# Transposes in 64 x 64 tiles and a static task graph in a talking-heads attention and feed-forward kernel

## The chip, the cores and the metric

The kernel runs on one core of a Trainium2 chip. The metric is device time in microseconds (us) of one execution, the lower the better; of several runs the median counts. TensorE is called PE in the profile (its weight loads PEld), VectorE DVE, ScalarE ACT, GpSimd POOL, SyncE SP.

## What is computed

Attention with "talking heads" (heads are mixed before and after the softmax), then a feed-forward layer with a squared ReLU:

```
q, k, v: (8, 12, 448, 64)    w_pre, w_post: (12, 12)    w_in: (768, 2048)    w_out: (2048, 768)
scores = q @ k^T / sqrt(64)                         # per batch and head
scores = einsum('bhij,hg->bgij', scores, w_pre)     # pre-mix over heads
attn   = softmax(scores, axis=-1)
attn   = einsum('bhij,hg->bgij', attn, w_post)      # post-mix over heads
x      = (attn @ v) as (8*448, 768)                 # tokens by heads*64
out    = relu(x @ w_in)**2 @ w_out                  # (3584, 768), float32
```

## The kernel before

**Stages of one batch.** POOL's queue issues the loads of q, k and v from HBM; they are cast to bf16 on the way. A token is number 4p + r: partition p of 112, place r of 4, so one source row of a head is 4 x 64 floats, 1024 bytes. TensorE transposes q and k (L635) with the identity as the moving operand: a task per pair of heads, 16 transposes of 112 x 64, the two heads of a pair on the two column halves of the array. The result is evicted to qkt, 64 features x 448 tokens, two heads on top of each other. QK (L768) gives scores of 12 chunks of 10 queries at a time, evicted to stage; a pair of heads is two matmuls of 448 columns, on the two row halves of the array. A move on SP's queue (L821, "rel", dring<-stage) rearranges each chunk of 10 queries x 12 heads into 120 partitions, in a ring of 12 slots. The pre-mix (L861) multiplies two chunks by a block matrix wk1 in four 64 x 64 tiles. ACT takes the exponential with the row sum (L884), DVE the reciprocal (L897), POOL folds it into the post weights wk2s (L905). The post-mix (L951) has the exponentials as stationary operand, 112 keys and 16 columns of padding at a time, and so gives the mixed attention with keys on partitions (a2t, evicted by L369 and L370). AV (L1023) sums over the four places r of the keys, 112 partitions each. Feed-forward: L1088 (F1) with ReLU at L1121 or L1122 and the square at L1131 (POOL or DVE), then L1180 (F2), eviction to osb, output by POOL's queue (L1245).

The first 100 queries of batch 0 take another way ("direct", L714): DVE and POOL scale the transposed q by w_pre (L686), and one matmul sums over heads; no move is needed.

**Tilings of the array.** QK, post-mix, F1 and F2 use two row halves ("row"), the pre-mix four quadrants ("quad"), transposes and AV two column halves ("cols"), direct and warm-up matmuls the full array ("full").

**What sets the order.** A planner in the kernel's own Python (class _Plan) runs while the program is built. TensorE's order is the string ORDER, written out by hand: each digit takes the next unit of one of ten streams (0 transposes, 1 QK, 2 pre-mix, 3 post-mix, 4 AV, 5 direct, 6 and 7 F1, 8 and 9 F2). The other engines take the ready task that can start first, with priorities; evictions go to ACT or DVE, whichever would end first by the planner's costs, squares to DVE or POOL. What comes out is a fixed order for each engine, with semaphores between them. PSUM has 8 banks that the planner hands out, oldest free first. Tasks appear in Python as the plan proceeds: a unit's "needs" and "go" create its followers, and the loads of batch 2 and later are released by a count of chunks (paced, GAP = 3). Transfers are reckoned with one time for loads and one for moves, and a fixed time that a move takes from running loads (STEAL). In the first 60 us warm-up matmuls (L598) are put where the planner sees a gap of TensorE, sized by that gap.

An F1 unit is half of a phase (6 matmuls), an F2 unit a quarter (8 matmuls); two phases make a group that holds two banks.

On POOL's queue at the start, the first four loads have a lower priority number than the identity (init2, L384), the other four a higher one; h0 is 0, 4, 8 or 10:

```
t_init2 = add("init2", POOL, fn_init2, [t_init], {POOL: (310.0, 400.0)}, -1e7 + 6)
-1e7 + h0 if b == 0 else b * 1000.0 - 1700.0 + h0
```

Of the kernel before, what the change touches and what calls it, by code (L numbers as in the profile page):

```python
# [6 lines left out]
AF = mybir.ActivationFunctionType  # L7
ALU = mybir.AluOpType
# [10 lines left out]
MODE_SWITCH = 108  # L19
ACT_BIAS = 14.5  # L20
STEAL = 560.0
INF = float("inf")
MERGE = False
ORDER = (
    "011051051501555115555555555551155551155551323332323233112111123323234322666767377667766662"
    "266766377662372777737733021112201121313313114181667666676627777776636666226687727738377277"
    "381281818118822188328338328388231991191192293991932242206163666361266616366362267667373777"
    "377220277117777177383383811411811866226688226686636633266661761716717277117777332777722779"
    "393329391191291912193820208322838338318318128224119122919339239121911913933230224333662206"
    "116616116626612263663636362277217737711177337173712277722778338224118118382218883932291919"  # L30
    "139139119329323818338222840081183181816362266662236663612266366363622771177173713171777222"
    "777737337382240028338318138118181228881238183181183282228993919339224339229199191391391192"
    "299392266326623636361316661161661622006316773227777331777171173771722277842833883118811822"
    "881832283893388138824229939222991939366116616362226677377636116166613636171711732777228737"
    "833772277421818118338118228838222883883228893391193911932299192239933919222941911933961163"
    "366226677166237716622667713771636226167373773722737738181838324228888338382228899822898398"
    "399339936677646777667676677676667686776867676777868777676777888667667766877667766999889889"
    "999999989999888"
# [12 lines left out]
class _Task:  # L51
# [3 lines left out]
                 "done", "bias", "sync")  # L55

    def __init__(self, name, engine, fn, deps, after, cost, prio, sem, seminc, mode, dma):
# [18 lines left out]
        self.done = False  # L76
        self.bias = 0.0
        self.succs = []
        self.avail = 0.0


class _Unit:

    __slots__ = ("mode", "go", "needs", "nbanks")

    def __init__(self, go, needs, nbanks=0, mode=None):
        self.mode = mode
        self.go = go
        self.needs = needs
        self.nbanks = nbanks  # L90


class _Plan:


    def __init__(self, nbanks):
        self.tasks = []
        self.ready = []
        self.free = {PE: 0.0, ACT: 1300.0, DVE: 400.0, POOL: 1400.0, SP: 800.0}
        self.per_engine = {e: [] for e in ENGINE_NAMES}  # L100
        self.committed = []
        self.streams = []
        self.mode = None
        self.load_free = 0.0
        self.move_free = 0.0
        self.loads = []
        self.bank_users = {i: [] for i in range(nbanks)}
        self.bank_age = {i: i for i in range(nbanks)}
        self.taken = set()
        self.age = nbanks  # L110
        self.keep_warm = lambda gap: None

    def add(self, name, engine, fn, deps=(), cost=None, prio=0.0, sem=None, seminc=0,
            mode=None, after=(), dma=None):
        t = _Task(name, engine, fn, deps, after, cost, prio, sem, seminc, mode, dma)
        t.order = len(self.tasks)
        self.tasks.append(t)
        t.nwait = 0
        for d in t.deps + t.after:
            if d.done:  # L120
                t.avail = max(t.avail, d.end + SEM_LAT if d in t.deps else 0.0)
            else:
                t.nwait += 1
                d.succs.append(t)
        if engine == PE:
            assert t.nwait == 0
            start = max(self.free[PE], t.avail)
            if t.mode != self.mode:
                start += MODE_SWITCH
                self.mode = t.mode  # L130
            self._commit(t, PE, start)
        elif t.nwait == 0:
            self.ready.append(t)
        return t

    def _commit(self, t, e, start):
# [4 lines left out]
        if t.dma:  # L141
            kind, service, piece = t.dma
            if kind == "load":
                self.load_free = max(self.load_free, start + 1200.0) + service
                t.end = max(start + held, self.load_free) + 1600.0
                self.loads.append(t)
            else:
                at = start + 900.0
                behind = self.load_free - at
                if behind > 0:  # L150
                    at += min(behind, 2000.0)
                    service += min(behind, 12.0 * max(
                        [45.0] + [x.dma[2] for x in self.loads if x.end > at]))
                    self.load_free += STEAL
                    self.loads = [x for x in self.loads if x.end > max(at, self.move_free)]
                    for x in self.loads:
                        x.end += STEAL
                self.move_free = max(self.move_free, at) + service
                t.end = self.move_free + 2200.0
        t.done = True  # L160
        self.per_engine[e].append(t)
        self.committed.append(t)
        for s in t.succs:
            s.nwait -= 1
            if t in s.deps:
                s.avail = max(s.avail, t.end + SEM_LAT)
            if s.nwait == 0:
                self.ready.append(s)

# [3 lines left out]
    def find(self, n, now):  # L173
        best = sorted((max(self.bank_time(i), now), self.bank_age[i], i)
                      for i in self.bank_users if i not in self.taken)
        if len(best) < n:
            return INF, ()
        return best[n - 1][0], [x[2] for x in best[:n]]

    def take(self, n):  # L180
        _, got = self.find(n, self.free[PE])
        self.taken.update(got)
        return got, [t for i in got for t in self.bank_users[i]]

    def give(self, banks, users):
        for i in banks:
            self.taken.discard(i)
            self.bank_users[i] = list(users)
            self.age += 1
            self.bank_age[i] = self.age  # L190

    def next_unit(self, order, at):
        if at >= len(order):
            return None
        s = self.streams[int(order[at])]
        u = s[0]
        needs = u.needs()
        if needs is None:
            return None
        now = self.free[PE]  # L200
        est = max([now] + [t.end + SEM_LAT if t.done else INF for t in needs if t is not None])
        if u.nbanks:
            est = max(est, self.find(u.nbanks, now)[0])
        if u.mode != self.mode:
            est = max(est, now + MODE_SWITCH)
        return (est, u, s) if est < INF else None

    def run(self, order=""):
        at = 0
        while True:  # L210
# [10 lines left out]
            f = self.next_unit(order, at)  # L221
            if f is not None and (best is None or f[0] <= best[0]):
# [1151 lines left out]
```

## Time and profile before

| | us |
|---|---|
| median of 3 runs | 564.76 (559.62 to 566.79) |
| the profiled execution's own time | 557.64 |
| its span, first to last instruction | 555.9 |
| PE busy | 523.0 |
| ACT busy | 428.7 |
| DVE busy | 380.2 |
| POOL busy (its DMA issues counted) | 249.0 |
| mean granted TensorE clock | 0.983 |

Busy times are unions of instructions, and the ends of matmuls are modelled, so start-to-start distances in the timeline say more about what a matmul costs than its own duration. In a line of a group, the name is line, engine, operation and "out<-in"; "idle before" is the engine's idle time in front of the group's instructions and what ended it. Digits of the clock row are tenths of full speed in 40 equal slices.

### The profile page before, as it was taken

To read this page: it belongs to the slowest core of one execution; us is meant where nothing else is said; L and a number is where in the kernel's file an instruction comes from. 1 tells how busy PE (TensorE), PEld (TensorE's weight loads), DVE (VectorE), ACT (ScalarE), POOL (GpSimd) and SP (SyncE) were. 2 spreads that over 40 slices of the span, in tenths; PEclk is the share of its full clock that TensorE was granted. 3 is DMA by queue.
4 is the path that set the end of the run, shared out by engine and by line. 5 is a ranking of instruction groups with operands and counts; after the bars stand their busy time and mean duration, and the time that the engine had idled before them with its cause. 6 is when DMAs were issued, how large, how long until landed. Compare 5 with 4: busy or idle time off the path is not lost.

```text
span 555.9 us, 22831 instructions
## 1 busy us (share of the span) xinstructions
PE 523.0 (94%) x9479; PEld 328.3 (59%) x9479; DVE 380.2 (68%) x872; ACT 428.7 (77%) x1212; POOL 249.0 (45%) x441
## 2 busy tenths in 40 slices
PE   7979999999599999999999989999999999999994
PEld 3436675687376564566557555566446554558872
DVE  5776866777297878876888757965597757834430
ACT  2877977998499989897888969888888987884220
POOL 7973546355383447622763534324432326522001
PEclk8989999999899999999999989999999999999998
DMA  8999999953976899746896897435834558342013
GB/s 106 173 228 229 162 166 176 215 124 49 173 161 139 163 161 169 148 97 125 147 186 117 145 186 162 87 58 125 168 56 89 133 122 157 63 99 59 3 31 86
DMA packets 95878, 72.85 MB, mean 131 GB/s; under 512 B 6192, under 2 KB 93440, under 8 KB 95776
## 3 DMA queue, kind: packets, MB, share of 16 engines
q0 software_dynamic: 49504, 33.43, 38.8%
q1 hardware_dynamic: 46128, 37.85, 29.9%
q8 instruction: 77, 1.26, 0.9%
q14 instruction: 25, 0.20, 0.1%
q10 hardware_dynamic: 144, 0.10, 0.1%
HBM read 45.70 MB, written 11.01 MB: 102 GB/s over the span
## 4 chain that ended last, share of the span: by engine, by line
PE 78%; DMA 9%; ACT 5%; DVE 3%; SPq 2%; issue 1%; POOL 0%; POOLq 0%; ACTq 0%
PE ps L1180 25%; PE ps L1088 23%; DMA dring<-stage 8%; PE ps L861 7%; PE ps L1023 7%; PE ps L951 6%; PE ps L768 5%; PE ps L635 3%; ACT pring L884 3%; SPq L821 2%; ACT stage L369 2%; DMA kraw<-in_k_dram 1%; DVE a2t L370 1%; DVE h1t L1122 1%; DVE h2t L1131 1%
## 5 line engine op out<-in xcount | busy, mean ns | idle before, releaser
L884 ACT ACTIVATE pring<-ps 128x448 bf16<-128x448 f32 x360 | 191.8, 553 | 22.3 <-PE ps L861 19.4
L1088 PE MATMUL ps<-xt,w_in_sb 64*128 64x448 bf16 (+2 forms) x2112 | 171.8, 299 | 1.9 <-PE ps L861 0.7
L1180 PE MATMUL ps<-w_out_sb,h2t 64*128 64x384 bf16 x1792 | 172.5, 324 | 0.0
L905 POOL TENSOR_TENSOR wk2s<-wk2b,rinv 128x120 bf16<-128x120 bf16 (+1 forms) x179 | 69.9, 392 | 159.6 <-DVE rinv L897 159.0
L370 DVE CAST a2t<-ps 112x480 bf16<-112x480 f32 (+1 forms) x196 | 120.7, 638 | 20.4 <-PE ps L951 19.1
L370 DVE CAST stage<-ps 120x448 bf16<-120x448 f32 (+2 forms) x186 | 108.7, 614 | 26.8 <-PE ps L768 20.3
L1088 PEld LDWEIGHTS ps<-xt,w_in_sb 64*128 64x128 bf16 x2112 | 95.2, 94 | 48.1 <-PE ps L861 5.3
L369 ACT ACTIVATE stage<-ps 120x448 bf16<-120x448 f32 (+3 forms) x186 | 94.5, 553 | 26.9 <-PE ps L768 21.7
L1180 PEld LDWEIGHTS ps<-w_out_sb,h2t 64*128 64x128 bf16 x1792 | 81.2, 94 | 54.5 <-issue 7.7
L369 ACT ACTIVATE a2t<-ps 112x480 bf16<-112x480 f32 (+1 forms) x172 | 93.8, 576 | 12.2 <-PE ps L951 10.6
L1131 POOL TENSOR_TENSOR h2t<-h1t 128x448 bf16<-128x448 bf16 (+2 forms) x101 | 75.7, 759 | 52.1 <-ACT h1t L1121 34.6
L884 ACT ACTIVATION_READ_ACCUMULATOR pring<-ps 128x1 f32 x360 | 78.3, 218 | 0.0
L951 PEld LDWEIGHTS ps<-wk2s,pring 60*128 60x128 bf16 x2880 | 59.8, 94 | 26.2 <-issue 2.6
L861 PE MATMUL ps<-dring,wk 64*64 64x448 bf16 (+1 forms) x700 | 58.0, 368 | 15.8 <-DMA dring<-stage 10.6
L1122 DVE TENSOR_SCALAR h1t<-ps 128x448 bf16<-128x448 f32 (+2 forms) x103 | 49.4, 496 | 29.7 <-PE ps L1088 28.7
L951 PE MATMUL ps<-wk2s,pring 60*128 60x60 bf16 x2880 | 66.8, 188 | 2.5 <-POOL wk2s L905 0.8
L1245 POOL DMA_DIRECT2D out_dram<-osb x54 | 33.7, 629 | 75.5 <-DVE osb L370 44.1
L768 PE MATMUL ps<-qkt 64*128 64x448 bf16 (+2 forms) x372 | 60.5, 356 | 2.2 <-DVE qkt L370 0.9
L897 DVE RECIPROCAL rinv<-rowsum 128x2 f32<-128x2 f32 (+1 forms) x184 | 29.0, 158 | 41.1 <-ACT pring L884 40.5
L1121 ACT ACTIVATE h1t<-ps 128x448 bf16<-128x448 f32 (+2 forms) x73 | 31.5, 441 | 26.1 <-PE ps L1088 25.8
L861 PEld LDWEIGHTS ps<-dring,wk 64*64 64x64 bf16 (+1 forms) x700 | 17.2, 104 | 46.6 <-issue 17.3
L1023 PE MATMUL ps<-a2t,vraw 112*64 112x220 bf16 (+1 forms) x768 | 41.5, 266 | 0.0
(50 smaller groups left out, 361.6 us busy)
## 6 DMA issues: line engine op xcount, KB each, us to landing
dring<-stage SPq DMA_DIRECT2D x342, 105.0 KB
vraw<-in_v_dram POOLq DMA_DIRECT2D x24, 224.0 KB, 6.6
qraw<-in_q_dram POOLq DMA_DIRECT2D x23, 224.0 KB, 6.8
kraw<-in_k_dram POOLq DMA_DIRECT2D x23, 224.0 KB, 8.1
w_in_sb<-in_moe_w_in_dram POOLq DMA_DIRECT2D x8, 384.0 KB, 15.0
w_out_sb<-in_moe_w_out_dram POOLq DMA_DIRECT2D x12, 256.0 KB, 37.7
out_dram<-osb POOLq DMA_DIRECT2D x8, 336.0 KB, 4.1
out_dram<-osb POOLq DMA_DIRECT2D x8, 288.0 KB, 4.2
```

Source lines behind the costliest of these rows:

```text
L369: return eng.activation(o, i_, AF.Copy)
L370: return eng.tensor_copy(o, i_)
L768: r_ = eng.matmul(ps[0:m, banks[par], 0:S], qkt[r0:r0 + 64, pb, p, 0, i0:i0 + m], qkt[r0:r0 + 64, pb, p, 1, :], start=True, stop=True,)
L861: r_ = eng.matmul(ps[64 * y:64 * y + 64, banks[x], 0:S], wk1[64 * x:64 * x + 64 - R0 * x, :], dring[64 * x:64 * x + 64 - R0 * x, (g0 + y) ...
L884: return eng.activation(pring[:, pr, 0:S], ps[:, bank, 0:S], AF.Exp, accum_out=rowsum[:, pr, :])
L905: return eng.tensor_tensor(wk2s[:, p0:p0 + n, :], i0.to_broadcast([128, n, PR]), rinv[:, p0:p0 + n, :].to_broadcast([128, n, PR]), ALU.mult)
L951: r_ = eng.matmul(pout(banks[x], jb, y, n), pring[64 * x:64 * x + PR, pr + y, jb * JB:jb * JB + 128], wk2s[64 * x:64 * x + PR, pr + y, :], ...
L1023: r_ = eng.matmul(ps[kk * 64:kk * 64 + 64, bank, x * n:(x + 1) * n], vraw[:, h, r, :], a2t[half][:, r, h, a0:a0 + n], start=(r == 0), stop ...
L1088: r_ = eng.matmul(ps[:, banks[x], 0:n], w_in_sb[64 * y:64 * y + 64, ft, t * 128:(t + 1) * 128], xt[64 * y:64 * y + 64, ft, c0:c1], start=( ...
L1122: return eng.tensor_scalar(h1t[:, s, 0:n], ps[:, bank, 0:n], 0.0, None, op0=ALU.max)
L1131: return eng.tensor_tensor(h2t[:, t16, o0:o0 + n], h1t[:, s, 0:n], h1t[:, s, 0:n], ALU.mult)
L1180: r_ = eng.matmul(ps[:, banks[hh], 0:FH], h2t[64 * y:64 * y + 64, t16, col:col + 128], w_out_sb[64 * y:64 * y + 64, t16, hh * FH:(hh + 1) ...
```

## The change

*Layout.* A token is number 7p + t: partition p of 64, place t of 7. The loads of q and k put heads 0 to 5 on partitions 0 to 63 and heads 6 to 11 on 64 to 127, two heads a load, with source rows of 7 x 64 floats (1792 bytes); v has places 0 to 3 on the lower and 4 to 6 on the upper partitions. In the program that is built, 144 loads of q, k and v are issued where there were 74. A transpose task holds four heads: 56 transposes of 64 x 64, in waves of four quadrants, so its tiling is "quad". The transposed keys are put in the order of POS, so that the post-mix can take 128 keys (two places t) as one stationary operand without padding; AV sums over 128 partitions, and one of the eight half-blocks of v is zero. QK always takes 128 queries. The output goes out in two pieces of 64 tokens for each tile.

*Planner.* All tasks are created before planning, banks belong to a group; the costs of TensorE's units are new constants; transfers are planned as two queues that share the DMA engines in proportion to their packets; a task's instructions are counted in blocks of 256, and a block that would be needed less than 4.0 us after the one before makes the task longer in the plan. The order of loads of later batches is set by "after" (planned after a given pre-mix), which sets an order and no semaphore.

*Units and order.* An F1 unit is a whole phase (12 matmuls), an F2 unit half a phase (16); ORDER is a new string. The matmuls of all kinds but the transposes (768 to 1344) and warm-up (27 to 40) keep their numbers. In the built programs, 49 of the full-width squares on POOL become 33 and 31 on DVE become 47. On POOL the identity comes behind all twelve loads of batch 0, whose numbers are -1e7 + 0, 2 and 4.

The diff's core:

```diff
-MODE_SWITCH = 108
+MODE_SWITCH = 106.0
-STEAL = 560.0
+BLOCK = 256
+FETCH = 4000.0
+DMA_START = {"move": 1420.0, "load": 1350.0}
+DMA_END = {"move": 1850.0, "load": 1700.0}
 ORDER = (
...
+    def fetch_wait(self, t, start):
+        before = self.instrs // BLOCK
+        after = (self.instrs + t.instrs) // BLOCK
+        if after == before:
+            return 0.0, None
+        part = (after * BLOCK - self.instrs) / t.instrs
+        at = start + part * t.cost[PE][0]
+        return max(0.0, self.fetched - at), at
...
-    RJ = 4
-    JB = S // RJ
+    PJ = 64
+    NT = S // PJ
+    NS = 4
+    POS = (1, 3, 5, 0, 2, 4, 6)
...
+    QUADS = ((0, 0), (1, 1), (0, 1), (1, 0))
...
-        qraw = sb("qraw", [JB, H, RJ, D], DT.bfloat16)
+        qraw = sb("qraw", [128, H // 2, NT, D], DT.bfloat16)
...
+        def load_qk(b, a, x, u, deps, after, prio):
+            raw, src = ((qraw, q), (kraw, k))[x]
+
+            def fn(eng, en):
+                i_ = bass.AP(src.tensor, (b * H + u * NP + 2 * a) * S * D,
+                             [[NT * D, PJ], [S * D, 2], [1, NT * D]])
+                eng.dma_start(raw[64 * u:64 * u + 64, 2 * a:2 * a + 2, :, :], i_).then_inc(
+                    sem_qk[a].handle, 16)
+
+            return plan.add("ldqk%d_%d_%d_%d" % (b, a, x, u), POOL, fn, deps,
+                            {POOL: (725.0, 0.0)}, prio, sem_qk[a], 16, after=after,
+                            dma=("load", 710.0, 88.0))
...
-                        for i, src in enumerate((qraw, kraw)):
-                            for r in range(RJ):
-                                for kk in range(2):
-                                    r_ = eng.transpose(
-                                        ps_bf[kk * 64:kk * 64 + 64, bank,
-                                              i * S + r * JB:i * S + (r + 1) * JB],
-                                        src[:, 2 * p + kk, r, :],
-                                        ident[0:JB, 0:JB],
-                                    )
...
-                               c_mm(2 * RJ, JB, 10.0), 0, "cols")
+                    for i, src in enumerate((qraw, kraw)):
+                        for t in range(NT):
+                            o = i * S + (POS[t] if i else t) * PJ
+                            for u, c in QUADS:
+                                r_ = eng.transpose(
+                                    ps_bf[64 * c:64 * c + 64, g.banks[u], o:o + PJ],
+                                    src[64 * u:64 * u + 64, 2 * a + c, t, :],
+                                    ident[64 * u:64 * u + 64, 64 * u:64 * u + 64],
+                                )
...
+                t_tr = unit(s_T, "tr%d_%d" % (b, a), fn_tr, qk_tasks[(b, a)] + [t_init2],
+                            14 * 32.0 + 36.0, "quad", g, 8 * NT)
...
-                         {SP: (815.0, 0.0)}, g * 1.0, sem_dsl[slot], 16, dma=("move", 620.0, 0.0))
+                         {SP: (815.0, 0.0)}, g * 1.0, sem_dsl[slot], 16, dma=("move", 470.0, 54.0))
...
+                    for s in range(NS):
+                        j0 = (2 * s + 1) * PJ % (NT * PJ)
+                        o0 = (y * NS + s) * PR
...
+                                pring[64 * x:64 * x + PR, pr + y, j0:j0 + 2 * PJ],
```

## The prediction

> **What bounds the kernel now.** I read the page first, then the waits of TensorE, then single instructions in the timeline, then stretches of the start. The page's busy shares, its clock row and one DMA queue (packets, MB, share of the engines):
>
> ```profile
> PE 523.0 (94%) x9479; PEld 328.3 (59%) x9479; DVE 380.2 (68%) x872; ACT 428.7 (77%) x1212; POOL 249.0 (45%) x441
> PEclk8989999999899999999999989999999999999998
> q8 instruction: 77, 1.26, 0.9%
> ```
>
> TensorE is the bound in nearly every slice; ACT and VectorE have a quarter to a third of their time free. So the end moves by what TensorE no longer does, plus what it no longer waits for. Its waits, longest in total first (us in total, times, longest):
>
> ```profile
> PE ps L861 <- DMA dring<-stage: 10.6, 5, 5.8
> PE ps L861 <- ACT pring L884: 2.9, 3, 1.1
> PE ps L635 <- DMA kraw<-in_k_dram: 1.9, 1, 1.9
> PE ps L951 <- POOL wk2s L905: 0.8, 2, 0.4
> ```
>
> Half of the roughly 22 us of idle is five waits of the pre-mix for the on-chip move (dring<-stage). They cost twice: after the longest the granted clock is halved. Two stretches (us, busy by engine, then PEclk):
>
> ```profile
> 142.00:149.00 7.00, 1.26 (x16) 0.49 (x13) 1.20 (x6) 2.19 (x8) 2.42 (x5) 0.96 1.10 173
> 149.00:152.00 3.00, 2.98 (x28) 1.73 (x30) 0.00 (x0) 1.16 (x4) 0.00 (x0) 0.53 0.79 179
> ```
>
> The same halving stands at 36 to 39 us (0.50) and 322.4 to 326 (0.53), each behind such a wait: about 1.4, 1.5 and 1.7 us lost, 4.6 us together. Waits on the move with their cold clock are thus 15.2 us.
>
> What a unit of work costs on TensorE, from its timeline (start, us, then the group):
>
> ```profile
> 172.17 0.39 PE L951 MATMUL ps<-wk2s,pring 60*128 60x60 bf16 x16
> 172.41 0.82 PE L1180 MATMUL ps<-w_out_sb,h2t 64*128 64x384 bf16 x8
> 173.16 0.38 PE L861 MATMUL ps<-dring,wk 64*64 64x448 bf16 x4
> 173.47 0.39 PE L635 MATMUL ps<-ident,qraw 112*64 112x112 bf16 x8
> 173.69 0.36 PE L635 MATMUL ps<-ident,kraw 112*64 112x112 bf16 x8
> 173.89 0.36 PE L635 MATMUL ps<-ident,qraw 112*64 112x112 bf16 x8
> ...
> 176.39 0.82 PE L1180 MATMUL ps<-w_out_sb,h2t 64*128 64x384 bf16 x8
> 177.05 0.39 PE L951 MATMUL ps<-wk2s,pring 60*128 60x60 bf16 x16
> 177.37 0.57 PE L861 MATMUL ps<-dring,wk 64*64 64x448 bf16 x8
> 177.87 0.82 PE L1180 MATMUL ps<-w_out_sb,h2t 64*128 64x384 bf16 x8
> ```
>
> Read from start to start. Eight transposes (four pairs) take 0.20 us, 0.049 a pair. An output unit of eight followed by its own kind of tiling takes 0.66 (176.39 to 177.05), but 0.75 in front of the pre-mix (172.41 to 173.16): a change of the array's tiling costs 0.09. Two pre-mixes take 0.50, less 0.09 that is 0.205 each, for 448 columns that four tiles stream at once. A post-mix of 16 takes 0.24 where no tiling changes, 8 pairs of 0.030.
>
> **Transposes.** Before: 768, 384 pairs at 0.049, 18.9 us, all on TensorE's path. After: 1344 in 336 waves of four. No row has a 64-column wave. Streaming 64 columns at the pair's rate (112 columns in 0.049 less 0.0025) is 0.027, so 0.029 is the low end: 9.8 us. The high end is two tiles at a time, like the post-mix's pairs of 60 columns, 0.060 a wave: 20.2 us. The new planner holds 14 x 32 + 36 ns for a task, 0.0346 a wave. Its other constants agree with the rows above (205 ns a pre-mix, 28 ns a post pair, 164 ns an output pair where the rows have 165), and the pre-mix shows four tiles at once; so I take 24 x 0.484 = 11.6 us: minus 7.3 (minus 9.1 to plus 1.3).
>
> [...]
>
> **Changes of tiling.** Counted in the orders of the two built programs, without the full-array ones: 243 before, 192 after, since transposes now share the pre-mix's tiling and units are longer. 51 x 0.09 = minus 4.6. Full-array changes go from 26 to 45 and idle-filling warm matmuls from 27 to 40, all in the first 60 us, where they stand in front of waits: 0 to 13 x 0.19 (a 448-column matmul, as a QK pair takes) + 19 x 0.09 = 4.2 if the waits aren't there; I take 1.0.
>
> **The start.** The identity is made on POOL, in its queue behind the first four loads; in the new order it stands behind all twelve. Now:
>
> ```profile
> 1.37 0.84 POOL L513 DMA_DIRECT2D qraw<-in_q_dram  x1 [0.86 <-POOLq L1359]
> 4.38 0.34 POOL L384 TENSOR_SCALAR_AFFINE_SELECT ident<-ident 128x128 bf16<-128x128 bf16 x1
> 5.33 0.66 POOL L513 DMA_DIRECT2D kraw<-in_k_dram  x1
> 8.15 0.39 PE L635 MATMUL ps<-ident,qraw 112*64 112x112 bf16 x8 [1.93 <-DMA kraw<-in_k_dram]
> ```
>
> 1.37 + 0.84 + 11 x 0.65 + 0.34 = 9.7 us, against 8.15 for the first transpose: 1.6 late. VectorE's scaling runs without a break from there to 20.1 us and the direct scores wait for it, so I take the 1.6 whole (0 if the second and third transposes, which now find their data landed, give it back).
>
> **POOL.** Loads of q, k, v go from 74 issues (54 us: 36.7 + 17.2) to 144. At 0.63 (the output's mean of 629 ns) to 0.73 that is 91 to 105 us, 37 to 51 more; 16 squares of 0.958 leave for VectorE (16 x 0.763 = 12 us there). POOL goes to about 50%, VectorE to 72%, neither the bound. The cover is POOL's idle time ahead of the folds (153 us); where it is gone, a fold, and the post-mix behind it, is late by one issue. Between 10 and 35 us, where twelve loads of the next batch stand among the first folds, it is thin: 0 to 3, I take 1.0.
>
> **Instructions.** 576 more transposes are 1152 more instructions of 64 bytes, 4.5 packets of the 77 of queue q8. TensorE has 0.7 us put down to "issue". The planner now reckons with 4.0 us a packet; the bound is one such wait: 0 to 4, taken 0.5. Evictions, QK, AV and the feed-forward matmuls keep their counts; rows beyond 112 partitions run in parallel, and no row shows a cost by partitions (88 and 120 rows evict in 612 and 615 ns): 0.
>
> **Waits.** The new order is another draw, made with a model in which loads and moves share the DMA engines. It could keep all 15.2 us, lose all, or double it. Batch loads become fewer packets (q and k from 21,504 to 12,288 rows of source), so the moves are disturbed for less time; I take a third off: minus 5.
>
> **Sum.** Own time of the profiled execution 557.6 (span 555.9): -7.3 -4.6 +1.0 +1.6 +1.0 +0.5 -5.0 = -12.8, gives 544.8. That execution lies 1.3% under the median of the runs shown (564.76); by the same ratio, 0.977, the median becomes 551.8.
>
> **The rivals.** All in the median's terms (own time x 1.013).
> *The waits stay* at 15.2 us: 549.8 own, 556.8. For it: such waits come from landing times that a planner guesses. Against: only five did, in eight batches.
> *The waits go*: 534.6 own, 541.4. For it: the rest of TensorE's idle time is waits under 2 us each.
> *The change doesn't do what it says*: the transposes run two tiles at a time (0.060): 553.4 own, 560.5. The post-mix pairs speak for it, the pre-mix's four at once against. [...]
> *The moves starve* (slower). A packet of the new q and k loads holds 1792 source bytes in place of 1024 and a move must let it pass; if each of the seven next batches brings a wait like that at 142.9 us (5.75 and 1.4 cold), 50 us stand in place of 15.2: 584.6 own, 592. It decides once the waits on dring pass 15.2 + 19 = 34 us, five of the longest. Speaking for it: at 138 to 143 us three v loads, a q and a k load ran beside 16 moves when the longest wait came. Against: fewer packets in all. [...]
>
> **How the numbers follow.** Forecast 0.44, waits stay 0.23, waits go 0.17, transposes don't gain 0.09, starved moves 0.07. Faster by over 2% (about what a measurement of this kernel can tell from no change) means under 553.5: all of "waits go", three quarters of the forecast, a fifth of "waits stay": 0.17 + 0.33 + 0.04 = 0.54. Slower: the starved moves, 0.07. Within 2%: 0.39. The range runs from just under "waits go" to just over "transposes don't gain", 539 to 563; outside are a part of the former, the starved moves and the ends of the bounds, about 0.2.
>
> **What would show it.** In the new trace: a task of 56 transposes starting its successor 0.48 us later (0.84 would be the rival); starts 0.3 us after pre-mixes into transposes falling to 0.2; the first transpose near 9.7 us and POOL's identity just before it; POOL at about half; waits for dring with their cold clock about 10 us in all. I am wrong if PE's total wait grows past 35 us, if TensorE stops inside transposes with "issue" as the reason, or if the folds become what the post-mix waits for.

## The result, and the profile after

| | before | after |
|---|---|---|
| time, median of 4 runs (us) | 563.12 (559.62 to 566.79) | 588.37 (583.95 to 592.63) |
| ratio, 95% interval | | 1.0447 (1.0329 to 1.0564) |
| profiled execution: own time / span (us) | 557.6 / 555.9 | 583.95 / 582.2 |

Medians are of all runs, while ratios and their intervals leave out runs over 1.5% above the fastest of their kernel, so that a ratio can differ a little from the quotient of two medians. The change makes the kernel 4.5% slower. Here are the lines of the new page that answer to those shown of before (busy shares, clock row, the queue of instructions); the line numbers are those of the changed kernel:

```profile
PE 525.3 (90%) x10068; PEld 325.5 (56%) x10068; DVE 387.3 (67%) x889; ACT 424.5 (73%) x1213; POOL 267.6 (46%) x493
...
PEclk9987999999999997999998999999999999999998
...
q8 instruction: 81, 1.33, 0.9%
```

TensorE is busy for 2 us more in a span that is 26 us longer: its share falls from 94 to 90%, and so do VectorE's and ScalarE's. No other engine became the bound; all of them wait more. These are TensorE's longest waits (us in total, times, longest):

```profile
PE ps L819 <- DMA dring<-stage: 24.3, 16, 4.0
PE ps L993 <- ACT stage L417: 3.4, 1, 3.4
PE ps L819 <- DVE stage L418: 3.4, 2, 2.6
```

The five waits of the pre-mix for the move (10.6 us) have become sixteen (24.3 us), and the evictions into stage (copies out of PSUM), which may not overwrite a row before its move has read it, wait too:

```profile
ACT stage L417 <- DMA dring<-stage: 9.0, 4, 3.6
DVE stage L418 <- DMA dring<-stage: 4.6, 3, 2.8
```

(before: 2.4 in 2 and 1.3 in 2). So the same queue holds TensorE directly and, through ScalarE and VectorE, a second time. Behind most of the long waits the granted clock (the column after the five engines) halves, as before. Two stretches of the start:

```profile
25.00:29.00 4.00, 0.07 (x1) 0.00 (x0) 0.45 (x2) 0.63 (x2) 0.73 (x2) 0.86 1.34 218
29.00:35.00 6.00, 5.95 (x36) 2.17 (x38) 1.36 (x3) 1.90 (x7) 2.13 (x4) 0.52 1.34 228
```

For 4 us nothing but one matmul runs on TensorE; the 6 us that follow are run at 0.52. Such half-clock stretches, without the one at the very end, add up to 27.3 us after and 13.7 before. An estimated half of that is lost: in the trace of after, at a granted clock of 0.5, the 228-column matmuls of F1 (L993) follow each other in 93 ns on average, at full clock in 49.

What the change was made for did come out. The start of TensorE's timeline:

```profile
9.04 0.41 PE L654 MATMUL ps<-ident,qraw 64*64 64x64 bf16 x28
9.29 0.40 PE L654 MATMUL ps<-ident,kraw 64*64 64x64 bf16 x28
```

28 transposes start their successors 0.25 us later, 0.0357 us for a wave of four (taken: 0.0346); over all of them, from start to the start of what follows and without gaps of over 60 ns, 14.2 us against 21.2 before. The first one stands at 9.04 (8.15 before, 9.7 forecast).

To see where the time went I split the span of each run into TensorE's gaps of over 60 ns, its warm-up matmuls (from start to next start, without such gaps), and half the length of its half-clock stretches but the last; the rest is its work at full clock with the tiling changes. All in us, worked out from the two traces, one execution each:

| | before | after | after 85 us: before | after 85 us: after |
|---|---|---|---|---|
| gaps over 60 ns | 25.7 | 49.5 | 15.2 | 32.0 |
| warm-up matmuls | 9.2 | 13.3 | 0 | 0 |
| half the half-clock time | 6.8 | 13.7 | 3.4 | 6.8 |
| these losses together | 41.7 | 76.5 | 18.6 | 38.8 |
| the rest of the span | 514.2 | 505.7 | | |

TensorE's own work is 8.5 us less, the losses are 34.8 us more: 14.5 in the first 85 us (23.1 to 37.6) and 20.2 behind them. Most of the gain that was forecast is there, and four times as much is given away in waits, warm-up matmuls and half clock. The experiments ask why.

### The profile page after: what moved, and what is told of

It is laid out like the page before. It is cut to its first block, busy times and chain, and to the rows that moved or that the text cites. A ratio compares the mean times of both kernels' runs of the same rounds, so it can differ in the third digit from the quotient of the medians.

```text
span 582.2 us, 24074 instructions
## 1 busy us (share of the span) xinstructions
PE 525.3 (90%) x10068; PEld 325.5 (56%) x10068; DVE 387.3 (67%) x889; ACT 424.5 (73%) x1213; POOL 267.6 (46%) x493
## 4 chain that ended last, share of the span: by engine, by line
PE 61%; DMA 17%; DVE 9%; SPq 7%; ACT 2%; issue 2%; POOL 1%; POOLq 0%; DVEq 0%
PE ps L1063 21%; PE ps L993 17%; DMA dring<-stage 16%; SPq L797 7%; PE ps L946 6%; PE ps L819 6%; PE ps L888 5%; PE ps L761 4%; DVE stage L418 3%; PE ps L654 2%; DVE a2t L418 1%; DVE h1t L1022 1%; DVE qkt L418 1%; DVE h2t L1031 1%; PE ps L714 1%
## 5 line engine op out<-in xcount | busy, mean ns | idle before, releaser
L993 PE MATMUL ps<-xt,w_in_sb 64*128 64x448 bf16 (+2 forms) x2112 | 171.2, 302 | 6.1 <-ACT stage L417 3.4
L1063 PE MATMUL ps<-w_out_sb,h2t 64*128 64x384 bf16 x1792 | 161.4, 323 | 0.0
L418 DVE CAST a2t<-ps 128x480 bf16<-128x480 f32 (+1 forms) x208 | 128.1, 638 | 36.1 <-PE ps L888 35.0
L993 PEld LDWEIGHTS ps<-xt,w_in_sb 64*128 64x128 bf16 x2112 | 95.9, 95 | 55.8 <-issue 3.9
L418 DVE CAST stage<-ps 128x448 bf16<-128x448 f32 x179 | 107.0, 615 | 29.9 <-PE ps L761 22.9
L417 ACT ACTIVATE stage<-ps 128x448 bf16<-128x448 f32 x193 | 99.5, 555 | 25.3 <-PE ps L761 15.4
L417 ACT ACTIVATE a2t<-ps 128x480 bf16<-128x480 f32 (+1 forms) x160 | 86.5, 569 | 20.4 <-PE ps L888 19.9
L819 PE MATMUL ps<-dring,wk 64*64 64x448 bf16 (+1 forms) x700 | 58.5, 368 | 32.4 <-DMA dring<-stage 24.3
L1031 POOL TENSOR_TENSOR h2t<-h1t 128x448 bf16<-128x448 bf16 (+2 forms) x83 | 58.5, 712 | 45.6 <-ACT h1t L1021 36.2
L761 PE MATMUL ps<-qkt 64*128 64x448 bf16 x372 | 60.6, 353 | 2.7 <-DVE a2t L418 0.6
L1022 DVE TENSOR_SCALAR h1t<-ps 128x448 bf16<-128x448 f32 (+2 forms) x92 | 45.2, 502 | 21.6 <-PE ps L993 19.7
L1021 ACT ACTIVATE h1t<-ps 128x448 bf16<-128x448 f32 (+2 forms) x84 | 36.4, 439 | 22.8 <-PE ps L993 21.5
L946 PE MATMUL ps<-a2t,vraw 128*64 128x220 bf16 (+1 forms) x768 | 43.1, 270 | 0.9 <-ACT a2t L417 0.9
```

Source lines behind the costliest of these rows:

```text
L417: return eng.activation(o, i_, AF.Copy)
L418: return eng.tensor_copy(o, i_)
L761: r_ = eng.matmul(ps[:, g.banks[x], 0:S], qkt[r0:r0 + 64, pb, p, 0, i0:i0 + IT], qkt[r0:r0 + 64, pb, p, 1, :], start=True, stop=True,)
L819: r_ = eng.matmul(ps[64 * y:64 * y + 64, gr.banks[x], 0:S], wk1[64 * x:64 * x + 64 - R0 * x, :], dring[64 * x:64 * x + 64 - R0 * x, (g0 + ...
L946: r_ = eng.matmul(ps[kk * 64:kk * 64 + 64, g.banks[0], x * n:(x + 1) * n], vraw[:, h, s, :], a2t[half][:, s, h, 0:n], start=(s == 0), stop ...
L993: r_ = eng.matmul(ps[:, g.banks[x], 0:n], w_in_sb[64 * y:64 * y + 64, ft, t * 128:(t + 1) * 128], xt[64 * y:64 * y + 64, ft, c0:c1], start ...
```

## The experiments

Runs of one kernel differ by some 4 to 9 us, and a split of losses is of one execution, so differences of a few us between two splits say little. Theory A: the moves from stage to dring land later beside loads than the new planner says, and the new order has no slack for it. Rivals: B, the order and the layout cost the time by themselves; D, the order at the start; E, wrong prices that put the other engines' work in a bad order.

**Loads taken away.** In both kernels q, k and v of batches 1 to 7 are loaded into 8 partitions only. The core of it in the changed kernel, for q and k (v likewise, and in the kernel before with 8 of its 112):

```diff
+                m = 8 if b else PJ
...
-                             [[NT * D, PJ], [S * D, 2], [1, NT * D]])
-                eng.dma_start(raw[64 * u:64 * u + 64, 2 * a:2 * a + 2, :, :], i_).then_inc(
+                             [[NT * D, m], [S * D, 2], [1, NT * D]])
+                eng.dma_start(raw[64 * u:64 * u + m, 2 * a:2 * a + 2, :, :], i_).then_inc(
```

> This is the changed kernel with the loads of q, k and v of batches 1 to 7 cut to 8 of their 64 partitions (the scores of those batches are then made of old data; order, instructions and waits are the same). Theory A, the moves from stage to dring land later than the planner says because they share the DMA engines with loads, and the new order has no slack for it: from batch 1 on the moves land within about 4 us of their issue (mean of all moves now 5.2), PE's waits for dring fall from 24.3 us to the 10 to 12 us that lie in the first 75 us, the waits for stage behind them go too, and the time falls from about 588 to 560 to 567, a ratio to before of 0.995 to 1.01. Rival B, the order and the layout cost the time by themselves (banks, evictions, exponentials), whatever the DMA does: 578 or more, a ratio of 1.025 or above.

> The kernel before with the same loads cut to 8 of their 112 partitions (old data from batch 1 on). Theory A: its 10.6 us of waits for dring lie for the most part in the later batches, so some 5 us go with the loads: ratio 0.985 to 0.995, and the few_loads kernel stays 0 to 2% behind it. Rival B: nothing here, 0.997 to 1.0, and few_loads stays 3% or more behind. If few_loads comes out ahead of this one, the changed kernel has the gain that was planned and loses it to transfers alone.

Measured: 574.24 us, ratio 1.0151 (1.0013 to 1.0289), for the changed kernel; 549.43 us, 0.9776 (0.9693 to 0.986), for the one before. Loads cost both much the same, some 3% and 2%, and between the two 3.8% stay. That is neither theory. The moves of the changed kernel now land 4.73 us after the start of their issue on average, where the plan has 4.67; behind the first 36, which are batch 0's, it is 4.34 for 4.61. And yet PE waits for them:

```profile
PE ps L821 <- DMA dring<-stage: 17.7, 14, 4.3
```

Of the 38.8 us of losses behind 85 us, 24.7 stay. So landing times beside loads explain only a part of it, and my first theory falls as the main cause. The moves are issued late. SP's row in the timeline, for the first twelve moves of batch 5 (start, length in us, count); first the changed kernel, then few_loads:

```profile
336.64 13.53 SPq L797 DMA_DIRECT2D dring<-stage  x12
```

```profile
324.78 13.25 SPq L799 DMA_DIRECT2D dring<-stage  x12
```

Twelve issues take 13.5 us, 1.13 each. The planner holds 0.815 for each (line 801), as the old one did. Sorted by their place in a row of issues without a pause (of 0.2 us), behind 85 us: the first takes 0.78 us, the second 0.83, the third and later ones 1.11 on average (1.07 in few_loads, 1.05 in the kernel before), and the spread is wide, 0.77 to 1.81 from the 5th to the 95th percentile. The last of twelve moves in such a row is thus issued some 3 us later than at the planner's price (1.9 to 5.5 us in the changed kernel), with or without loads. In the changed kernel's chain that ended last it looks like this (start, length, what):

```profile
297.51 0.81 SPq L797
298.32 0.04 issue
298.36 1.14 SPq L797
299.50 0.04 issue
299.54 0.84 SPq L797
300.38 0.04 issue
300.42 6.07 DMA dring<-stage
...
306.96 0.55 ACT stage L417
307.50 0.05 issue
307.55 2.22 PE ps L993 x12
```

Issues in a row, a landing, an eviction into the row of stage that it frees, and only then the feed-forward matmuls: no engine's work is on this path for 9 us.

**The start.** One pre-mix unit is moved behind the direct scores in the order (the rest of it is the same):

```diff
-    "0010555115511111555555555525355511111535232152215311322333133344422772332223663622636363"
+    "0010555115511111555555555553555111115352321522152311322333133344422772332223663622636363"
```

> The changed kernel with one pre-mix unit, the first, moved behind all the direct-score units in TensorE's order; that unit waits 3.98 us at 25 us now and the clock halves behind it. Theory A: the wait moves on to the pre-mixes behind it, since the moves of batch 0 set the pace there (a planner with the measured landing times gives the same span within 0.5 us): ratio 1.035 to 1.05, as the change itself. Rival D, the start's order is what is wrong (13.5 us are lost in the first 45 us): 6 to 10 us come back, ratio 1.025 to 1.035.

Measured: 585.51 us, 1.0427 (1.0321 to 1.0534). The 3.98 us wait at 25 us is gone, and one of 5.2 us at 34 to 40 us stands in its place, for an eviction into stage that itself waited for a move. Moving this one step doesn't take the loss away.

**Prices mended, the order kept.** The planner's moves get the start and the rate of the trace, TensorE's order stays:

```diff
+            if kind == "move":
+                busy = sum(x[1] for x in self.moving["load"] if x[0] <= at)
+                at += min(BEHIND, busy)
...
+            rate = {id(x): 1.0 if len(on) == 1 else SHARE[0] if x is a else SHARE[1]
+                    for x in on}
```

> The changed kernel, TensorE's units in the same order, with the planner's moves priced as the trace has them (2.85 us more before the first packet where loads are queued, and 0.42 of the rate beside loads). The planner then orders ScalarE's, VectorE's and GpSimd's tasks anew and puts in more warm-up matmuls in the first 60 us. Theory A, the order of TensorE's units is what has no slack: only a few us come back, 572 to 583, ratio 1.015 to 1.035. Rival E, the wrong prices hurt through the other engines' order: 563 or less, ratio 1.00 or less.

Measured: 590.98 us, 1.045 (1.0273 to 1.0626): nothing comes back, less than either theory gave it. TensorE takes its units in the order that is written out; a planner that knows better can only fill its gaps (63 warm-up matmuls for 40).

**The moves made small.** Two runs with moves cut from batch 1 on: to 2 of 12 heads (few_packets, the first block), or to 64 of 448 columns (narrow_moves, the second, with the same old lines).

```diff
-                eng.dma_start(dring[R0:R0 + nv * H, slot, :],
-                              stage[r0:r0 + nv, n % 2, :, :]).then_inc(sem_dsl[slot].handle, 16)
+                m = 2 if b else H
+                eng.dma_start(dring[R0:R0 + nv * m, slot, :],
+                              stage[r0:r0 + nv, n % 2, 0:m, :]).then_inc(sem_dsl[slot].handle, 16)
...
+                w = 64 if b else S
+                eng.dma_start(dring[R0:R0 + nv * H, slot, 0:w],
+                              stage[r0:r0 + nv, n % 2, :, 0:w]).then_inc(sem_dsl[slot].handle, 16)
```

> The changed kernel; from batch 1 on each move takes 2 of the 12 heads (20 pieces of 896 bytes for 120), so that dring keeps old rows for the others; order, instructions and waits are the same. The first four runs leave this: with few loads the moves land as fast as planned (4.73 us against 4.67) and PE still waits 22 us for dring, because SP issues the moves of one stage tile slower than the planner's 0.815 us: 0.79 and 0.84 us for the first two of a row, 1.08 on average from the third on, in every run, so the twelfth is issued 2.5 us late. Theory A2, that pace comes from the pieces of a move and is what the order has no slack for: issue 0.77 to 0.82 us throughout from batch 1 on, and 12 to 20 us come back: 563 to 572, ratio 1.00 to 1.02. Rival F, the pace is SP's own (0.95 to 1.08 us still): 575 to 584, ratio 1.02 to 1.04.

> The changed kernel; from batch 1 on each move takes 64 of the 448 columns (120 pieces of 128 bytes: as many pieces, a seventh of the bytes), old columns for the rest. Theory A2: the pace of issue is set by the number of pieces, so it stays at 1.0 to 1.1 us from the third on, and only the landing gets shorter: 574 to 582, ratio 1.02 to 1.035. If it is set by the bytes that are still in flight, the pace falls to 0.8 us and the time is that of few_packets or less: ratio 1.00 to 1.02.

Measured: few_packets 549.29 us, 0.9774 (0.9712 to 0.9836); narrow_moves 552.43 us, 0.9842 (0.9776 to 0.9907). Both come back further than any expectation. The same twelve issues, few_packets and then narrow_moves:

```profile
315.80 9.70 SPq L798 DMA_DIRECT2D dring<-stage  x12
```

```profile
315.71 9.97 SPq L798 DMA_DIRECT2D dring<-stage  x12
```

0.81 and 0.83 us each, about the planner's price. So the pace is not SP's own (F falls), and it isn't the number of pieces either, which narrow_moves keeps: it goes with the bytes that a move carries. With it the waits go (few_packets):

```profile
PE ps L820 <- DMA dring<-stage: 7.0, 3, 4.1
```

and these three lie in the first 63 us, where the moves are whole. Of the losses after 85 us, 38.8 us, 7.6 are left. That the moves cost the changed kernel those 31 us is shown. This cut doesn't tell the pace of issue from the landing, which gets shorter too (4.81 us to 2.70 on average behind the first 36 moves); few_loads speaks for the pace, since there the landing was as short as planned and most of the loss stayed. That the time now is near the 551.8 us of the forecast is chance: the forecast was for whole moves and kept 10 us of waits.

**The same cut in the kernel before.**

> The kernel before with the same cut: from batch 1 on a move takes 2 of the 12 heads, old rows for the rest. Theory A2, the old order had slack for the moves and the new one has not, while the rest of the change is worth what the sum said (transposes and tilings about 11 us): this kernel gains only its own waits for dring of the later batches and the clock behind them, 3 to 6 us, ratio 0.985 to 0.995, and the changed kernel with the same cut (0.977) stays 1 to 2% ahead. Rival G, the change is worth nothing even where moves cost nothing: ratio 0.970 to 0.980 here, level with the changed kernel.

Measured: 538.43 us, 0.9615 (0.9516 to 0.9715). More than I gave it, by far, and outside both expectations: the kernel before loses 17.7 of its 18.6 us behind 85 us to the moves as well, not the 3 to 6 that I took from its waits for dring alone. And with small moves it is 1.6 to 2% ahead of the changed kernel. Most of the difference lies at the start, where both kernels still move whole rows: losses by 85 us are 23.8 us here and 38.2 in few_packets. Behind 85 us the changed kernel has 6.7 us more of losses and, over the whole span, 7.3 us less of work. So two places remain to be told apart: the later batches, which the moves explain, and the first 85 us.

**The start again: loads of w_in taken away.** Six fills of 0.5 replace most of w_in's load:

```diff
-                                          [[FF, 128], [128 * FF, NFT], [1, WC]])
-                            dst = w_in_sb[:, :, c0:c0 + WC]
+                                          [[FF, 16], [128 * FF, NFT], [1, WC]])
+                            dst = w_in_sb[0:16, :, c0:c0 + WC]
```

> The changed kernel with w_in loaded into 16 of its 128 partitions (the rest of w_in_sb is filled with 0.5 by six instructions of ScalarE and VectorE before 9 us, where both are idle; the rest of the planned schedule is the same to the nanosecond). Batch 0's moves, planned to land in 5.2 us, land in 9.06 while the loads of w_in are queued, and by 85 us the changed kernel has lost 43 us to gaps, warm-up matmuls and half clock (the kernel before: 27). Theory A2, batch 0's moves are late through the loads beside them: moves 1 to 36 land in 4.5 to 6.5 us, the loss by 85 us falls to 31 to 36, ratio 1.02 to 1.035. Rival D2, the start's own order (the first pre-mix so early, banks, evictions) is the cause: the loss stays at 40 to 43, ratio 1.04 to 1.05.

Measured: 587.68 us, 1.0433 (1.0334 to 1.0531); the loss by 85 us is 39.4, against 37.6 in the changed kernel and 23.1 in the one before. (The 43 and 27 of the expectation add the modelled durations of the warm-up matmuls, which overlap.) By the time that is D2's case, but the run doesn't settle it. The fills ran 3 us longer than planned and held VectorE's first eviction, the clock halved behind that (0.88 granted on average by 85 us, 0.92 in the changed kernel), and the first move was issued at 23.0 us instead of 20.1. From there on the changed kernel falls 9.6 us behind its plan until the pre-mix of chunk 24, this one 4.5 us, and its first twelve moves land in 5.0 us for 8.6. So the loads beside them do slow the first moves, and about 5 us of the start hang on that; what was regained was lost again, in part before 85 us, and behind it there is no gain either (gaps of 30.8 us and 24 us of half clock). How much of the start's 14.5 us is due to the loads stays open.

**An order made with the right prices.** If the order is what has no slack, then the same changed kernel with another order must be fast. The prices in the planner were mended (those of late_moves; 1.075 us for an issue from the third of a row on; VectorE's squares at 1.93 times their price, since those of 448 columns take 604 ns and were planned at 313), and the order was searched anew by small exchanges, starting from the changed kernel's. The core of it:

```diff
+        if t.dma and e == SP:
+            self.row = self.row + 1 if start - self.free[SP] < 200.0 else 0
+            if self.row > 1:
+                held = ISS
```

> The changed kernel with the planner's prices for a move mended (1.075 us for the issue of a move from the third of a row on, 2.85 us more to its first packet behind queued loads, 0.42 of the rate beside loads) and the squares of VectorE at 1.93 times their price, and with an order of TensorE's units searched anew under these prices, starting from the changed kernel's order; its planned span is 532.1 us, as the old plan's 532.9. Nothing else is changed. Theory A2, the loss comes from an order made with wrong prices for the moves: the plan holds within 2 to 3%, 545 to 556, ratio 0.965 to 0.99. Rival H, the loss is in what the change does (layout, loads, tilings) or in things that no price covers: it stays above 575, ratio over 1.02.

> As r_nomargin, but the order was searched with another 0.6 us on the landing of each move, planned span 533.5 us. Theory A2: slack is what was missing, so this one is as fast or faster than r_nomargin though its plan is 1.4 us longer: 541 to 552, ratio 0.96 to 0.98, PE's waits for dring under 8 us. Rival H: above 575, ratio over 1.02.

Measured: r_nomargin 555.38 us, 0.9881 (0.9779 to 0.9984); r_margin 557.02 us, 0.9887 (0.9791 to 0.9983). Rival H falls: layout, loads, tilings and the number of moves are those of the changed kernel, only order and prices differ, and 5.4% come back. r_nomargin's wait for the move:

```profile
PE ps L834 <- DMA dring<-stage: 4.2, 6, 1.4
```

24.3 us of waits for the move have become 4.2, although an issue from the third on takes 1.11 us as before. Its plan holds better, though not within the 2 to 3% expected: the span is 4.0% over the planned 532.1 us, where the changed kernel's is 9.3% over. The margin brought nothing that can be measured (r_margin's waits for dring are 3.7 us), and r_margin missed its range. Both medians of ratios lie 1.1 to 1.2% under the kernel before, with intervals that end just below 1; their losses (45.3 and 42.7 us) are still 1 to 4 us above its 41.7. Not tried: the same search with the old prices, which would tell the prices from a lucky draw, and each mended price alone (the squares' price was mended with the moves').

Searched further, with the time between two packets of instructions at 4.6 us for 4.0 as well:

> As r_nomargin, searched further, with 0.3 us on the landing of each move and 4.6 us in place of 4.0 for the time between two packets of TensorE's instructions (r_nomargin had waits for them of 1.2, 2.4 and 1.7 us between 52 and 67 us); planned span 531.4 us. Theory A2, what is left behind the plan is what the prices still miss, mainly at the start: 547 to 555, ratio 0.975 to 0.985, no gap named issue over 1.5 us. If the order's remaining losses are not in these prices: as r_nomargin, 0.985 to 0.992.

> As r_margin, searched further, with 0.6 us on the landing of each move and the same 4.6 us for instructions; planned span 532.4 us. Theory A2: 546 to 555, ratio 0.972 to 0.985; if the remaining losses are not in these prices: as r_margin, 0.985 to 0.992.

Measured: r2_small 554.51 us, 0.9858 (0.98 to 0.9916); r2_margin 555.26 us, 0.9861 (0.981 to 0.9911). Not to be told from r_nomargin: the intervals overlap for most of their length, and both ratios lie in the range for losses that are not in these prices. In r2_small the direct wait for the move is all but gone, but it has in part changed places:

```profile
PE ps L834 <- DMA dring<-stage: 1.2, 3, 0.7
PE ps L834 <- DVE stage L433: 5.3, 2, 3.4
DVE stage L433 <- DMA dring<-stage: 8.3, 5, 3.6
```

The two longest-lasting of these waits of TensorE, 5.3 us together and ended at 164 and 280 us, are for an eviction into stage that itself waited for a move. Its gaps named issue still reach 2.4 us, so that half of the expectation failed. Most of what is left of its losses (39.7 us) lies at the start: 13.3 us of gaps and 12.3 of warm-up matmuls by 85 us. r2_small has the lowest median of these four, 1.4% under the kernel before; four orders searched with the mended prices came out at 0.986 to 0.989.

**What paces the issues.** A whole move adds 11 times to its semaphore, the counter that tells of its landing. Theory K below is set against a theory J, that the pace goes with what each row of stage has to give, 12 pieces in a whole move; by J half_rows, with 12 pieces a row, stays at 1.0 to 1.1 us and a ratio of 1.02 to 1.045, and half_heads, with 6, comes to 0.78 to 0.85 us and 0.98 to 0.995. Two runs with the same 60 pieces of 896 bytes, from batch 1 on, half_rows (first block) and half_heads (second, with the same old lines):

```diff
-                eng.dma_start(dring[R0:R0 + nv * H, slot, :],
-                              stage[r0:r0 + nv, n % 2, :, :]).then_inc(sem_dsl[slot].handle, 16)
+                m = 5 if b and nv == CH else nv
+                eng.dma_start(dring[R0:R0 + m * H, slot, :],
+                              stage[r0:r0 + m, n % 2, :, :]).then_inc(sem_dsl[slot].handle, 16)
...
+                m = 6 if b else H
+                eng.dma_start(dring[R0:R0 + nv * m, slot, :],
+                              stage[r0:r0 + nv, n % 2, 0:m, :]).then_inc(sem_dsl[slot].handle, 16)
```

> The changed kernel; from batch 1 on each move takes 5 of its 10 rows of stage (60 of 120 pieces of 896 bytes; old rows in dring for the rest). What is open is what sets the 1.05 to 1.11 us of an issue. A whole move adds 11 times to its semaphore, not 16, and no more than 10 or 11 of its pieces are under way at once. [...] Theory K, the bytes or pieces of the whole move set it: half of them, 0.78 to 0.85 us, ratio 0.98 to 0.995.

> The changed kernel; from batch 1 on each move takes 6 of the 12 heads of all its 10 rows (60 pieces of 896 bytes as in half_rows, old rows for the rest). [...] Theory K: the same pace and time as half_rows.

Measured: half_rows 565.88 us, 1.0113 (1.0065 to 1.0161), with 6 additions to the semaphore and 0.98 us an issue from the third on; half_heads 551.44 us, 0.9804 (0.9747 to 0.986), with 11 additions and 0.80 us. TensorE's waits, half_rows and then half_heads:

```profile
PE ps L820 <- DMA dring<-stage: 13.1, 8, 4.4
```

```profile
PE ps L820 <- DMA dring<-stage: 7.7, 3, 4.3
```

Same bytes, same pieces, 2.6% apart by the medians: K falls. The packets' times fit J: no more than 5 of half_rows' pieces are under way in 97% of the time that any is, and no more than 10 of a whole move's in 98%, as many as the rows that the move takes. The pace goes with how much one row has to give: 12 pieces of 896 bytes in half_rows as in a whole move, 6 in half_heads. It isn't the count of pieces alone, since narrow_moves has 12 of 128 bytes for each row and is fast (0.83 us). J holds in kind and missed both of its ranges for half_rows, by 0.02 us in the pace and a percent in the time; its pieces also run a little faster (58 ns on average for 64), which may be why.

## Why the prediction was wrong, step by step

**Transposes, minus 7.3: right.** Start to start, with the tiling changes behind them, they give back 7.0 us (21.2 to 14.2); the wave of four is 0.0357 where I took 0.0346. Four tiles run at once, 0.0357 over four is 9 ns a transpose, and the rival of two at a time (0.060) is out.

**Tilings, minus 4.6, full-array and warm matmuls, plus 1.0, instructions, plus 0.5.** TensorE's work without gaps, warm-up and half clock is 8.5 us less, where transposes and tilings gave 11.9. With 7.0 of it in the transposes, only some 1.5 is left for the other changes of tiling less the full-array ones; the 4.6 is not shown. Warm-up matmuls are 4.1 us more (9.2 to 13.3), where my upper bound had 2.5 for them: at the start one takes 0.33 us on average (13.3 over 40), more than the 0.19 us I gave it. Of instruction packets (16,384 bytes each) 81 came for 77, where I had 4.5 more.

**Start, plus 1.6: right up to the first transpose (plus 0.9), wrong as a picture of the start.** I followed the identity and ended there. By 85 us the new kernel had lost 14.5 us more than the old one.

**POOL, plus 1.0:** 46% busy, not half, and none of TensorE's longer waits is for a fold.

**Waits, minus 5: this is the step that failed.** It should have been some plus 30: gaps plus 23.8, half clock plus 6.8, about a third of it in the first 85 us. I wrote that "the new order is another draw", and took a third off because the loads became fewer packets. The draw isn't neutral. An order that is searched until the planner's span is short can use up whatever time the planner thinks free; where the planner prices a move too low, the pre-mix can come to stand just there. The new planner priced batch 0's moves at 5.2 us from issue to landing where they took 9.06 (the old one 9.7 for 9.6), later ones at 4.61 for 4.81 (the old one 6.26 for 5.71), and dropped the old one's surcharge for moves behind loads. Both hold 0.815 us for an issue that takes 1.05 to 1.11 in a row. Slack in the plans, from the planned landing of its last row to the planned start of a pre-mix, is under 0.5 us for 14 of 179 pre-mixes before and for 31 after. Thin slack alone is not the fault, since r_nomargin's plan has 27 such pre-mixes and loses little: it hurts behind a price that is too low. The old plan is 543.3 us against a span of 555.9 on the chip, which is 2.3% over; the new one 532.9 against 582.2, 9.3% over. I had compared both kernels' constants where they agreed with the trace (pre-mix, post-mix, output), not where they priced what TensorE waits for. The trace of before had the price of an issue in it, just ahead of the longest wait at 149 us, 0.99 us for each of sixteen:

```profile
134.80 15.85 SPq L821 DMA_DIRECT2D dring<-stage  x16
```

What is shown is that the moves, with the order around them, cost this time (few_packets, r_nomargin). That the search with low prices made the order bad is argued from the plans and the four searches with mended prices; the control, a new search with the old prices, is missing.

**The rival "moves starve" came nearest in time (592) and wrong in mechanism.** It wanted larger load packets to hold up the moves. The packets did grow (12,288 of 896 bytes as written for q and k, where all those loads came in 512), and behind queued loads the first packet of a move comes late, before as after (3.44 to 3.57 us after its issue ended, for 0.65). But the moves are not slower than before (5.23 us on average against 6.10), and with the loads of seven batches all but gone the changed kernel was still at 1.015. Its sign came about all the same: the waits for dring with their cold clock are 24.3 and some 12 us, past the 34 I gave, and TensorE's total wait of 49.5 us is past 35.

## What to carry to other kernels

When a change brings a new order and a new planner, compare the planner's constants with the trace first for the thing that the bound engine waits for, not for the thing that was improved: a search can turn a price that is too low into a wait. An engine with a fixed order can't use a gap (in late_moves, with the order kept, nothing came back), so slack ahead of a transfer is part of the order's cost; ask for each transfer how far the plan's landing is from its first use. The issue of a transfer can cost more in a row than alone (here 1.1 us for 0.78); measure a row of issues, not one.

## What the runs showed of the hardware

- The issue of a move on SP took 0.78 us for the first of a row (0.77 to 0.82 in all kernels with whole moves but r2_margin, with 0.91), 0.79 to 1.00 for the second and 1.05 to 1.13 on average from the third on, for 105 KB in 120 pieces of 896 bytes. With 120 pieces of 128 bytes, or 20 of 896, it took 0.77 to 0.79 in every place. With 60 pieces of 896 bytes it took 0.98 from the third on where they lay in 5 rows of stage, 0.80 where they lay in 10. A move from 10 rows adds 11 times to its semaphore, one from 5 rows 6 times, and one from 4 rows 5 times, one more than the rows each time. So the pace goes with what one row has to give: 12 pieces of 896 bytes with 0.98 and more, 6 with 0.80, 12 of 128 bytes or 2 of 896 with 0.77 to 0.79. Why it does is not shown: twelve pieces of 64 ns, one after the other, are an estimated 0.77 us, not 1.05 to 1.13.
- The first packet of a move came 0.65 us after its issue ended where no load was queued (after at 85.8 us), and 3.44 to 3.57 us after it where loads were (before at 19.5 and 71.0 us, after at 20.1 and 37.7 us). From 26 to 58 us of the kernel before, with both queues active, 116 packets of moves and 261 of loads were begun in a microsecond; loads alone, from 20 to 23 us, came to 341.
- Of the seven waits of over 1.7 us on TensorE in the changed kernel behind the first transposes, five go with 3.4 or 6.8 us at half the granted clock (at 28, 48, 100, 219 and 308 us), which costs an estimated 1.7 or 3.4 us again; two, of 2.57 and 1.81 us at 425 and 479 us, came without.
